# Later steps for batch 1's first-stage matmuls, an earlier step for M, in a kernel of an FFT filter and a two-branch maxout layer

## The chip, the cores and the metric

The kernel runs on one core of one Trainium2 chip. The core has a matrix engine (TensorE, PE in the profile, whose weight loads are PEld), a vector engine (DVE), a scalar engine (ACT), GpSimd (POOL) and a queue engine that only starts transfers (SP). Sixteen DMA engines move data between HBM and the on-chip memory SBUF. Matmuls write to PSUM, from which DVE or ACT copy ("evict") the result. Each engine executes its own instructions strictly in the order written, so one instruction that waits holds up all behind it on that engine. The metric is the device time of one execution in microseconds, as the median of several.

## The reference

```python
X = np.fft.rfft(x, axis=1)                    # x: 8 batches, 3072 rows, 256 channels
Y = X * (filt_r + 1j * filt_i)[None]
y = np.fft.irfft(Y, n=3072, axis=1)
x = y.reshape(24576, 256)
h1, h2 = x @ w1, x @ w2                        # 256 -> 1024
out = np.maximum(h1, h2) @ w_out               # 1024 -> 256
```

The kernel writes the maximum as max(h1, h2) = relu(h1 - h2) + h2. With Wd = w1 - w2 the first part needs one matmul into the hidden layer instead of two, and the second part is linear, so that h2 @ w_out = y @ M with M = w2 @ w_out, a 256x256 matrix that is made once.

## The kernel before

The transform of 3072 points is split into 96 x 32. Four stages make up the filter. The first multiplies with a 96-point table over the row index p (`f1` for batch 1, `s1` for batches 2 to 7, which fold pairs of rows first). The second (`s2`) does the 32-point part and the twiddle factors; its result is multiplied with the filter F (`product`, on DVE). The third (`s3`) goes back, and the fourth (`s4`) undoes the 96-point part and leaves y, transposed, for 384 rows at a time: one tile. Between the first and the second stage the data change their place across partitions by a round trip through DRAM: `f1` or `s1` store to `ad` (line 332 for batch 1, line 356 for others), and `f1_read` (line 338) or `s1_read` (line 362) reads it back as `bt`. Between the third and the fourth stage `zd` and `zr` do the same. Batch 0 alone goes through transposes on TensorE instead of these trips, in a prologue of about 38 us.

After the prologue comes one long loop over 64 tiles of 384 rows (8 per batch) and, in each tile, 8 steps. A step of the loop issues, in this order:

1. `moe_h(tt, j)`: two matmuls (line 448) that make the hidden block j of tile tt, and its eviction with the relu (line 450 on DVE or 452 on ACT);
2. what the table `mid` holds for this step: the visits, which do second and third stages of the next batch and first stages of the one after;
3. `moe_o(tt - 1, ...)`: three or four matmuls (line 480 with Wo, line 478 with M) into the output of the tile before;
4. what the table `todo` holds for this step, in the order in which it was planned;
5. after step 4 of a tile, `s4` (line 428) for the next tile.

Steps are numbered through a batch, 0 to 63; tile 0 has steps 0 to 7, in which there is no `moe_o` as no tile is before it. The planner is a list written out by hand: there are no costs or due times in it, and nothing is moved at run time.

What the change touches, all for the first two tiles and a little behind:

- `f1(1, c)` for c = 4 to 15: one matmul of 512 columns with C1 (line 324) on half of an input tile `xb`, an eviction to `at` (ACT, line 329, for even c; DVE, line 327, for odd c), and after each odd c a store of two c's to `ad` on SP. The calls for c = 0 to 3 stand before the loop. Input comes in three loads of POOL (line 88): c = 4 to 7 in `load_x(1, 2, 2)`, c = 8 to 11 in `load_x(1, 4, 2)`, c = 12 to 15 in `load_x(1, 6, 2)`. POOL issues the first, then the load of Wo (`load_wo`, line 288), then makes three quarters of Wd (line 292), and only then issues the other two, the last quarter of Wd and the casts of w2 (line 285).
- `prep_t(0)`, `prep_t(1)` at steps 7 and 8 transpose w2 (line 299, eviction on ACT, line 300), and `prep_m` multiplies it with Wo: 16 matmuls (line 306) and one eviction (line 308). M is first read by the last matmuls of an output block of tile 0, in `moe_o` at step 12.
- `f1_read(1)`: two transfers on SP that read `bt` of batch 1, each half of the frequencies; they wait for all stores to `ad`. The first second-stage matmuls of batch 1 (line 376) are in the visit at step 25, and they need the first of the two halves.
- `load_xf(2, c)`: the input of batch 2 in pieces, each two transfers on SP (line 93), and for c < 3 two small ones in between (line 97). `fold(2, c)` on POOL (lines 103 and 104) reads it, and `s1(2, c)` (line 349) at steps 25, 28, 31, ... reads the fold.

PSUM tiles for all but the output come from one ring of six (`ps`): an allocation waits for the eviction of the sixth before it.

Of the kernel before, what the change touches and what calls it, by code (L numbers as in the profile page):

```python
# [26 lines left out]
def kernel(  # L27
# [637 lines left out]
    def plan(b, step, fn, *a):  # L665
        todo.setdefault((b + step // 64, step % 64), []).append((fn, a))

    def plan_f1(b, nb, steps, read):
        for c, n in zip(range(4, 16), steps):
            plan(b, n, f1, nb, c, S if c % 2 == 0 else V)  # L670
        plan(b, read, f1_read, nb)
# [3 lines left out]
    def plan_f2(b, steps, quads, xs, folds):  # L675
        for n, st in enumerate(steps):
            mid.setdefault((b, st), []).append((visit, (b + 1, n, quads[n])))
        plan(b, steps[3] + 3, z_read, b + 1, 0)
        plan(b, steps[6] + 3, z_read, b + 1, 1)
        if b + 2 < B:  # L680
            for c in range(8):
                plan(b, xs[c], load_xf, b + 2, c)
                plan(b, folds[c], fold, b + 2, c)
            plan(b, steps[-1] + (6 if b else 11), s1_read, b + 2)
# [1 line left out]
    plan(0, 2, t2, 1, (V,))  # L686
    plan(0, 7, prep_t, 0)
    plan(0, 8, prep_t, 1)
    plan(0, 10, prep_m)
    for c in range(2, 8):  # L690
        plan(0, 8 * (c - 2) + 8, t2, c, (V,))
    plan_f1(0, 1, (1, 2, 5, 6, 9, 9, 10, 10, 11, 11, 12, 12), 13)
    plan_f2(0, (25, 28, 31, 35, 38, 42, 46), ((0,), (1,), (2,), (3,), (4,), (5,), (6, 7)),
            (9, 10, 14, 18, 21, 27, 30, 33), (16, 19, 25, 28, 31, 34, 38, 42))
    for b in range(1, B - 1):
        plan_f2(b, (7, 14, 18, 24, 31, 38, 42) if b > 1 else (14, 18, 24, 30, 34, 39, 42), ((0, 1), (2,), (3,), (4,), (5,), (6,), (7,)),
                range(-32, 32, 8) if b > 1 else range(-25, 31, 7), range(-22, 42, 8) if b > 1 else range(-15, 41, 7))
# [48 lines left out]
```

## Time and profile before

| | us |
|---|---|
| median of 3 runs | 503.3 (503.06 to 504.27) |
| the profiled execution, its own time | 506.75 |
| its span, first to last instruction | 504.9 |
| PE busy | 489.5 (97%) |
| DVE / ACT / POOL busy | 331.4 / 308.1 / 257.8 |
| loop starts (first `moe_h` on PE) | 38.66 |

Times below are microseconds from the start of the span of the profiled execution. In a timeline a line gives the start, the length, the engine, the line of the program, the operation and its tiles, and in brackets how long the engine sat idle before it and what released it. In a table by windows each row is one stretch: its length, the busy time of each engine with the number of instructions in brackets, then the clock that TensorE was granted as a share of full speed, the share of the DMA engines that was busy, and GB/s. Matmuls are pipelined, so the end of one and the start of the next overlap in the timeline; the distance from start to start is what a matmul costs in a stream.

### The profile page before, as it was taken

The numbers are of one execution on the slowest core, as the hardware profiler recorded it, in microseconds if no ns is written. First come the engines' busy times: TensorE is split into PE (matmuls) and PEld (weight loads), VectorE is DVE, ScalarE is ACT, GpSimd is POOL, SyncE is SP. The second block draws the span as 40 slices with busy tenths as digits, with TensorE's granted clock in tenths as the row PEclk, the third lists the DMA queues.
The fourth block names the chain that finished last, engine by engine and source line by source line (L and its number), as shares of the span: only waits on it lengthen the run. The fifth ranks groups of instructions, "written<-read, shape, count | busy, mean of one in ns | idle before, by whom it ended". The sixth has DMA issues, their size and how long they took to land.

```text
span 504.9 us, 13075 instructions
## 1 busy us (share of the span) xinstructions
PE 489.5 (97%) x5297; PEld 363.4 (72%) x5300; DVE 331.4 (66%) x514; ACT 308.1 (61%) x629; POOL 257.8 (51%) x342
## 2 busy tenths in 40 slices
PE   7788999999999999999999999999999999999996
PEld 3555767777777777777777777777777777777775
DVE  7785678557775687557764687557765687554552
ACT  5875477746774576547774676647774465544442
POOL 6695279566663755646645746528632221222220
PEclk9888999999999999999999999999999999999999
DMA  8989689997799659886779659796659235511112
GB/s 129 148 231 187 190 264 279 276 269 223 217 257 276 188 179 244 239 227 198 201 235 275 191 176 258 211 258 191 199 177 250 86 109 157 167 64 64 64 64 83
DMA packets 77966, 97.19 MB, mean 192 GB/s; under 512 B 8018, under 2 KB 54355, under 8 KB 77843
## 3 DMA queue, kind: packets, MB, share of 16 engines
q1 hardware_dynamic: 64642, 66.73, 49.5%
q0 software_dynamic: 13264, 29.64, 20.4%
q8 instruction: 41, 0.67, 0.6%
q14 instruction: 19, 0.15, 0.1%
HBM read 53.87 MB, written 47.19 MB: 200 GB/s over the span
## 4 chain that ended last, share of the span: by engine, by line
PE 90%; DMA 4%; POOL 3%; DVE 1%; issue 1%; ACT 0%; POOLq 0%
PE po L480 34%; PE ph L448 33%; PE po L478 8%; PE pz L399 5%; PE py L428 4%; DMA xb<-in_x_dram 3%; PE pa L349 2%; PE px L376 2%; POOL pq L382 1%; POOL xb L88 1%; PE pr L553 1%; PE pa L324 1%; DMA F<-in_filt_i_dram 1%; DVE F L130 0%; DVE pq L382 0%
## 5 line engine op out<-in xcount | busy, mean ns | idle before, releaser
L480 PE MATMUL po<-Wo,gt 128*128 128x256 bf16 x1536 | 261.0, 273 | 0.0
L452 ACT ACTIVATE gt<-ph 128x384 bf16<-128x384 f32 x321 | 157.0, 496 | 146.4 <-PE ph L448 145.7
L461 POOL DMA_DIRECT2D out_dram<-ot x186 | 102.6, 555 | 182.3 <-DVE ot L492 179.6
L480 PEld LDWEIGHTS <-gt 128*128 128x128 bf16 x1536 | 146.6, 98 | 66.0 <-issue 10.3
L450 DVE TENSOR_SCALAR gt<-ph 128x384 bf16<-128x384 f32 x191 | 104.9, 553 | 67.0 <-PE ph L448 63.8
L382 DVE TENSOR_TENSOR pq<-px,F 128x1024 bf16<-128x1024 f32 x91 | 106.9, 1218 | 23.2 <-PE px L376 22.7
L448 PEld LDWEIGHTS <-Wd 128*128 128x128 bf16 x1024 | 96.9, 98 | 12.4 <-issue 1.1
L103 POOL TENSOR_TENSOR xb<-XF 128x512 bf16<-128x512 f32 x48 | 61.2, 1275 | 45.6 <-DMA XF<-in_x_dram 35.5
L492 DVE COPY ot<-po 128x512 f32<-128x512 f32 x95 | 65.1, 685 | 25.2 <-PE po L480 24.1
L104 POOL TENSOR_TENSOR xb<-XF 128x512 bf16<-128x512 f32 x48 | 61.0, 1271 | 0.0
L353 ACT ACTIVATE at<-pa 128x512 bf16<-128x512 f32 x96 | 51.8, 610 | 2.4 <-PE pa L349 2.1
L403 ACT ACTIVATE zt<-pz 128x512 bf16<-128x512 f32 x84 | 45.6, 595 | 11.9 <-PE pz L399 9.7
L428 PE MATMUL py<-G,zr 96*128 96x96 bf16 x512 | 33.1, 207 | 0.2
L428 PEld LDWEIGHTS <-zr 96*128 96x128 bf16 x512 | 29.3, 98 | 2.7 <-DVE zr L556 0.4
L399 PE MATMUL pz<-pq,VP 64*64 64x256 bf16 x336 | 22.2, 281 | 0.1
L376 PE MATMUL px<-bt,U 64*64 64x256 bf16 x384 | 19.9, 275 | 1.2 <-ACT VQ L273 0.7
L399 PE MATMUL pz<-pq,VQ 64*64 64x256 bf16 x336 | 21.0, 269 | 0.0
L399 PEld LDWEIGHTS <-VP 64*64 64x64 bf16 x336 | 9.8, 105 | 13.6 <-issue 13.3
L349 PE MATMUL pa<-xb,CT 64*64 64x512 bf16 x192 | 19.5, 383 | 0.0
L376 PEld LDWEIGHTS <-U 64*64 64x64 bf16 x384 | 10.4, 107 | 4.1 <-issue 3.9
L563 PE MATMUL pd<-W 128*128 128x512 bf16 x28 | 10.5, 489 | 1.6 <-DVE zero L145 1.5
L349 PEld LDWEIGHTS <-CT 64*64 64x64 bf16 x192 | 8.7, 105 | 2.1 <-ACT gt L452 1.2
(429 smaller groups left out, 606.1 us busy)
## 6 DMA issues: line engine op xcount, KB each, us to landing
out_dram<-ot POOLq DMA_DIRECT2D x186, 128.0 KB, 3.4
XF<-in_x_dram SPq DMA_DIRECT2D x96, 192.0 KB, 5.1
ad<-at SPq DMA_DIRECT2D x56, 192.0 KB, 3.7
bt<-ad SPq DMA_DIRECT2D x14, 768.0 KB, 9.2
zd<-zt SPq DMA_DIRECT2D x42, 256.0 KB, 2.6
zr<-zd SPq DMA_DIRECT2D x56, 192.0 KB, 5.2
WS<-in_moe_w_dram SPq DMA_DIRECT2D x4, 512.0 KB, 7.1
xb<-in_x_dram POOLq DMA_DIRECT2D x8, 192.0 KB, 7.0
```

What stands on the lines that cost most here:

```text
L103: G.tensor_tensor(t_[:, 0], f[:, 0], f[:, 1], OP.add)
L104: G.tensor_tensor(t_[:, 1], f[:, 0], f[:, 1], OP.subtract)
L353: S.activation(at[:, m0:m0 + 2], pa[g], AF.Copy)
L382: E.tensor_tensor(pq, px.rearrange("p (o i) d -> p o i d", o=1).to_broadcast([128, 2, 2, D]), F[:, :, 2 * v:2 * v + 2, s], OP.mult)
L399: TE.matmul(pz[g][64 * s:64 * s + 64, i], tab[64 * g:64 * g + 64, 2 * v + i, s], pq[s][64 * g:64 * g + 64, q, i], start=(q == 0), stop=(q ...
L428: TE.matmul(py[:, m], zr[b][:, 4 * i + m, 128 * dc:128 * dc + 128], G1, start=True, stop=True)
L448: TE.matmul(ph, Wd[:, dc, 128 * j:128 * j + 128], y_[:, dc], start=(dc == 0), stop=(dc == 1))
L450: V.tensor_scalar(gt[tt][:, j], ph, 0.0, None, OP.max)
L452: S.activation(gt[tt][:, j], ph, AF.Relu)
L461: E.dma_start(out=dst, in_=ot[tt // 2][:, 3 * (tt % 2) + c])
L480: TE.matmul(p_, g_[:, n - 2, blk], Wo[:, n - 2], start=(e == 0), stop=(e == 9))
L492: V.tensor_copy(ot[tt // 2][:, e - 1:e + 1], po[q // 2 % 2])
```

## The change

The twelve first-stage calls of batch 1 that stand in the loop go from steps 1, 2, 5, 6, 9, 9, 10, 10, 11, 11, 12, 12 to steps 4, 5, 6, 7, 10, 10, 11, 11, 12, 12, 13, 13. The read of the exchange goes from step 13 to step 14. `prep_m` goes from step 10 to step 9. The first three pieces of batch 2's input are loaded at steps 10, 11 and 15 and no longer at 9, 10 and 14. What is computed, and on which engine, stays the same.

```diff
-    plan(0, 10, prep_m)
+    plan(0, 9, prep_m)
     for c in range(2, 8):
         plan(0, 8 * (c - 2) + 8, t2, c, (V,))
-    plan_f1(0, 1, (1, 2, 5, 6, 9, 9, 10, 10, 11, 11, 12, 12), 13)
+    plan_f1(0, 1, (4, 5, 6, 7, 10, 10, 11, 11, 12, 12, 13, 13), 14)
     plan_f2(0, (25, 28, 31, 35, 38, 42, 46), ((0,), (1,), (2,), (3,), (4,), (5,), (6, 7)),
-            (9, 10, 14, 18, 21, 27, 30, 33), (16, 19, 25, 28, 31, 34, 38, 42))
+            (10, 11, 15, 18, 21, 27, 30, 33), (16, 19, 25, 28, 31, 34, 38, 42))
```

## The prediction

> **What bounds the kernel now.** I read the page first: PE is busy 97% of the span, and the windows from 60 us on show it at 100%, so time is won only where PE stands still or runs slowly, and what is won there lasts unless something further on is late. Then the waits of PE from the loop's start to 80 us, to find the places; then windows of 3.41 us for the clock; then the timelines of PE and SP around the steps that move, and the transfers' times to landing.
>
> ```profile
> PE 489.5 (97%) x5297; PEld 363.4 (72%) x5300; DVE 331.4 (66%) x514; ACT 308.1 (61%) x629; POOL 257.8 (51%) x342
> ...
> PE pa L324 <- DMA xb<-in_x_dram: 2.2, 1, 2.2
> ...
> 8.49:11.90 3.41, 1.72 (x18) 0.69 (x15) 3.23 (x11) 1.83 (x6) 1.14 (x3) 0.99 1.07 181
> 11.90:15.31 3.41, 3.41 (x27) 2.29 (x27) 1.36 (x2) 2.81 (x6) 1.57 (x3) 0.51 1.10 178
> ...
> 18.72:22.13 3.41, 2.52 (x94) 1.91 (x92) 3.11 (x5) 3.41 (x7) 2.33 (x6) 1.00 1.03 138
> 22.13:25.55 3.42, 1.20 (x78) 0.79 (x56) 3.21 (x3) 2.79 (x6) 2.22 (x3) 0.99 0.96 171
> 25.55:28.96 3.41, 2.75 (x108) 1.71 (x98) 3.09 (x3) 2.24 (x5) 3.41 (x2) 0.51 0.87 196
> ...
> 39.20:42.61 3.41, 1.21 (x11) 0.63 (x9) 0.88 (x3) 0.89 (x2) 3.41 (x5) 0.99 1.17 140
> 42.61:46.02 3.41, 3.41 (x22) 2.18 (x21) 2.79 (x5) 1.17 (x3) 2.51 (x5) 0.51 1.14 265
> ```
>
> The wait is `f1(1, 4)` of step 1: its load lands at 41.7, and PE has stood since 39.55. The windows show a second cost. Three times a window in which PE was busy for 1.72 us or less is followed by one at a granted clock of 0.51; after a window with 2.52 busy the clock stayed at 1.00. The stall of step 1 is one of the three. From 42.01 to 47.06 PE took 5.05 us for work that at the full-clock distances takes 3.39 (six `ph` pairs at 0.326, one transpose group 0.445, three `f1` at 0.217, `py` 0.34): 1.66 us lost.
>
> The queue that matters later is SP, and the first use of what it reads:
>
> ```profile
> 51.31 0.30 SPq L332 DMA_DIRECT2D ad<-at  x1
> 51.66 0.42 SPq L93 DMA_DIRECT2D XF<-in_x_dram  x1
> 52.13 0.44 SPq L97 DMA_DIRECT2D XF<-in_x_dram  x1
> ...
> 54.25 0.32 SPq L332 DMA_DIRECT2D ad<-at  x1
> 54.62 0.43 SPq L93 DMA_DIRECT2D XF<-in_x_dram  x1
> ...
> 56.62 0.83 SPq L332 DMA_DIRECT2D ad<-at  x2
> 60.07 1.35 SPq L338 DMA_DIRECT2D bt<-ad  x2
> ...
> DMA to landing us min/median/max: 5.7/6.9/8.0
> ...
> 66.39 0.41 PE L376 MATMUL px<-bt,U 64*64 64x256 bf16 x8
> ```
>
> The first half of `bt` lands at 60.07 + 5.7 = 65.77, and PE uses it at 66.39: 0.62 us of slack, in a stretch where PE is full. Anything that brings PE here earlier without bringing `bt` earlier ends in a wait.
>
> **The change part by part.** Start PE at 39.39, where the next matmul could follow the first two `ph`.
>
> *Step 1 to 4, c = 4.* Now `ph` of steps 2, 3, 4 and the transposes of step 2 come before it: 3 x 0.326 + 0.445 = 1.42 us of work, until 40.81. Their inputs are there: POOL has the third quarter of Wd, which step 4 needs, at 40.24 (36.50 + 3.74), and the ring's six-back evictions end at 39.45 or before. The load is not earlier, since POOL's order isn't touched, so `f1(1, 4)` still starts at 41.75. The stall shrinks from 2.20 to 0.78 us: 1.42 won. In the window 39.20 to 42.61 PE is then busy 1.21 + 1.42 = 2.63, above the 2.52 that kept the clock: 1.66 won more.
>
> *Steps 5 to 8.* `py`, `ph`, `f1`, `ph`, `f1`, `ph`, transposes of w2, `f1`, and `ph` of tile 1 run at full clock from 41.97 to 44.72. Steps 6 and 7 need the last quarter of Wd (POOL, 42.49), step 7 the first cast of w2 (43.44): both there. ACT and DVE have two or three evictions of 0.5 to 0.7 queued, within the ring. Then `moe_o` of step 8 needs Wo. It was issued at 35.56 and took 9.9, so it lands at 45.46; the kernel before came here at 47.83 and never saw it. New stall: 0.78 us (bounds: nothing if Wo takes as long as its neighbours' 6.7 to 7.9, 1.3 if half a microsecond more; I take its own row). PE is busy 2.6 us in that window, so the clock should hold.
>
> *M a step sooner.* The second transposes of w2 now run at 45.94, ACT's copy (1.03) ends at about 47.6, and `prep_m` starts there, about 0.1 behind what PE could do: 0.1 lost. Its 16 matmuls (1.75) and M's eviction are the same work; M is ready at 50.2, two steps before its use. The first pair of step 10, `f1(1, 8)` and `(1, 9)`, starts at 50.16 against 49.92 before, since it now stands behind `prep_m`; its load landed at 40.16 + 7.1 = 47.3, the next at 40.68 + 7.9 = 48.6. No wait.
>
> *Sum to step 14:* 1.42 + 1.66 - 0.78 - 0.1 = 2.2 us won. Step 14's `ph`, at 56.69 before, comes at about 54.45.
>
> *SP.* Here the gain is given back. The store of c = 8, 9 was issued 1.39 after its matmuls began, so it now goes at 51.55 against 51.31. Behind it SP issues, in the same order as before, the four transfers of batch 2's piece 0 (1.85 us), a store, the four of piece 1 (1.9), two stores and the read: moving loads and stores by a step each keeps them in line. The 0.74 in which SP waited for the store of c = 10, 11 (54.25) goes, as that eviction is now done by 52.7. So the last store goes out at 56.63 instead of 57.06: only 0.43 earlier, although PE is 2.2 earlier. With the landing as before (some 2.95) the read is issued at 59.64 and its first half lands at 65.35. PE is there at 66.39 - 2.2 = 64.2. New stall: 1.2 us, and the gain there is 1.0 (bounds: 0.8 less stall if the read takes 0.5 to 0.8 less, because POOL's output writes of 59.43 and 60.0 are over sooner; 2.6 more if it takes the 8.3 of the fastest later read, in a fuller stretch; I take its own 5.7 with a little off).
>
> *What comes back after that.* Before, DVE was still at a copy and a relu when `px` was ready: product at 67.25, 0.86 after `px` began, against 0.43 at 74.34. PE then lost some 0.3 us at 69.64, waiting for it. With a PE stall ahead, DVE is free: 0.3 comes back, so 1.3.
>
> *Batch 2's piece 2*, a step later behind the same read, is issued right after it and lands the same 0.43 earlier. Its fold ended at 73.65 and `s1(2, 2)` used it at 74.56, a slack of 0.9; with the 0.43 that caps the gain there at 1.3, or 1.8 if the read is 0.5 faster. Pieces 0 and 1 are folded on POOL 5 us ahead of use, so the later issue costs nothing; without that cover a piece would cost the 2.5 us of a fold. Later exchanges have 2.4 us (batch 2: read at 102.93, landing up to 11.8, use at 117.30) and 4 us of slack (batch 3), so what is left reaches the end.
>
> So 1.3 by the rows as they stand, up to 1.8 with a somewhat quicker read; I take 1.5. On the profile's own 506.75 that is 505.25. The median of the runs shown is 3.45 lower; 1.85 of the 506.75 lies outside the span, and where the rest is the trace doesn't say. I take the difference over: 503.3 - 1.5 = 501.8.
>
> **Rule against row.** The row is the stall of 2.2 us with the clock at 0.51 in the window behind. The Trainium skill, "TensorE: Matmul & The Clock Gate", section on why this matters for your kernels, says to avoid idle gaps above about 3 us, which would leave a 2.2 us gap without a price. The windows here disagree: 1.7 to 2.2 us of idle in 3.41 sufficed three times. By that rule the sum to step 14 would be 0.54.
>
> **Rivals.**
> 1. *The read is quick, and nothing catches up.* All 2.2 stay: 501.1. For it: PE's whole gain is measured rows, and the read of `bt` has 0.26 MB less output traffic beside it. Against: slack 0.62.
> 2. *The clock is lost again, at step 25 (the other side).* A stall of 1.2 leaves PE busy 2.2 of 3.41 us, between the 1.72 that lost the clock and the 2.52 that kept it, so no row decides. It does from about 1.7 of idle at the latest. Price: 1.66. At that point: 2.2 - 1.7 + 0.3 - 1.66 = -0.9, so 504.2; at a stall of 1.2, 503.6.
> 3. *The half clock of 42.6 has another cause and stays, or is absent in unprofiled runs.* Then 1.42 - 0.78 - 0.1 = 0.54 is won; PE reaches step 25 within the slack, no new stall: 502.8. Against: the three pairs of windows. (This is also where the Trainium skill's rule above would put the time.)
> 4. *Wo lands later or earlier,* 44.7 to 46.8: it moves the first sum by +0.8 to -1.3, but step 25 takes up nearly all of it, so it changes little: counted within the forecast.
>
> **How the numbers follow.** A 0.3% change, 1.5 us, is about what a measurement of this kernel can tell from none. Forecast (won 1.0 to 1.9) 0.5; rival 1, 0.2; rival 2, 0.2; rival 3, 0.1. The range leaves out the worse half of rival 2 and holds the rest: 500.9 to 503.8. The forecast alone is 501.4 to 502.3. Faster by over 0.3%: 0.3 of the forecast, whose middle lies on the line, and all of rival 1: 0.5. Slower by over 0.3%: rival 2 with a stall beyond 2 us, or a read as long as the later ones: 0.13. Within: 0.37.
>
> **What would show it.** Right: PE's wait at line 324 falls to about 0.8 at 41.75 and the clock stays at 1.00 through 47; a wait of about 0.8 for Wo at line 480 at 45.5; step 14 about 2.2 earlier; SP's last store near 56.6 and a wait of 0.8 to 1.2 for `bt` at line 376 near 65. Wrong: the clock at 0.5 anywhere behind 38 us, no wait at line 376, or a `bt` read of over 7 us for its first half.

## The result

| | before | after |
|---|---|---|
| median of 22 runs each, us | 503.41 (501.77 to 506.40) | 505.29 (503.54 to 508.69) |
| ratio after / before | | 1.0039, 95% interval 1.0022 to 1.0056 |
| profiled execution, its own time, us | 506.75 | 504.60 |
| its span, us | 504.9 | 502.8 |

The kernel became slower by 0.39%, about 1.9 us. The forecast was 501.8, faster by 0.3%. The two profiled executions show the opposite sign: the span after is 2.1 us shorter. Both facts are true, and the way from one to the other is what this case teaches. Two executions timed later, one of the kernel before at 1005.08 us and one of xf_early at 1752.72, were far slower than all others and stand outside every ratio and count below.

The views of the profile after that answer to those shown of before: PE's busy line, the waits of PE, windows of 3.41 us (length; busy us of PE, PEld, DVE, ACT, POOL with counts; granted clock; DMA share; GB/s), SP's timeline with the landing of the two halves of the read, and the first use of `bt`.

```profile
PE 487.1 (97%) x5297; PEld 361.1 (72%) x5300; DVE 331.3 (66%) x514; ACT 308.3 (61%) x629; POOL 259.4 (52%) x342
...
PE px L376 <- DMA bt<-ad: 2.0, 1, 2.0
...
PE po L480 <- DMA Wo<-in_moe_w_out_dram: 0.5, 1, 0.5
...
PE pa L324 <- DMA xb<-in_x_dram: 0.4, 1, 0.4
...
39.20:42.61 3.41, 2.96 (x28) 1.76 (x28) 2.50 (x5) 2.63 (x7) 3.41 (x4) 1.00 1.24 248
42.61:46.02 3.41, 2.90 (x33) 2.35 (x32) 1.64 (x3) 2.34 (x4) 0.84 (x4) 1.00 1.06 236
59.07:62.48 3.41, 3.09 (x29) 2.20 (x26) 1.30 (x2) 1.71 (x4) 3.39 (x5) 1.00 0.59 170
62.48:65.89 3.41, 1.68 (x22) 1.17 (x23) 1.77 (x4) 1.01 (x3) 0.99 (x2) 1.00 1.13 353
65.89:69.30 3.41, 3.29 (x50) 2.28 (x48) 2.47 (x3) 3.00 (x8) 0.00 (x0) 1.00 1.08 323
...
49.52 0.30 SPq L332 DMA_DIRECT2D ad<-at  x1
49.87 0.42 SPq L93 DMA_DIRECT2D XF<-in_x_dram  x1
...
51.83 0.35 SPq L332 DMA_DIRECT2D ad<-at  x1
52.23 0.43 SPq L93 DMA_DIRECT2D XF<-in_x_dram  x1
...
54.21 0.83 SPq L332 DMA_DIRECT2D ad<-at  x2
58.90 1.18 SPq L338 DMA_DIRECT2D bt<-ad  x2
...
DMA to landing us min/median/max: 5.3/6.3/7.4
...
64.21 0.41 PE L376 MATMUL px<-bt,U 64*64 64x256 bf16 x8 [2.04 <-DMA bt<-ad]
```

The load wait of 2.2 us at line 324 is 0.4, the clock stays at 1.00 through 46, a wait of 0.5 us for Wo is new, and PE now waits 2.04 us for `bt` at step 25. These are the effects that were forecast; the last was forecast at 1.2. So the suspicion falls on the profiled execution of before: it may not stand for the rest.

The way to see it in a span is to cut it at two marks: the first `ph` of the loop on PE, and the first `px` of step 25. From the second mark to the end ten of these thirteen executions take 438.5 to 438.7 us, and up to the first mark all these kernels issue the same instructions; the loop's start alone lies anywhere from 37.0 to 40.6 us.

| execution | loop start | first `px` of step 25 | start to `px` | `px` to end |
|---|---|---|---|---|
| before (the page shown ahead) | 38.66 | 66.39 | 27.7 | 438.5 |
| b_again (kernel before) | 38.52 | 62.42 | 23.9 | 438.6 |
| b_look2 (kernel before) | 38.14 | 61.92 | 23.8 | 438.6 |
| b_look3 (kernel before) | 40.64 | 64.35 | 23.7 | 438.6 |
| after | 37.00 | 64.21 | 27.2 | 438.6 |
| after_again (kernel after) | 37.26 | 65.59 | 28.3 | 439.8 |
| late8 | 38.89 | 69.70 | 30.8 | 438.7 |
| first4 | 38.46 | 63.01 | 24.6 | 439.5 |
| first4_again (first4) | 40.31 | 64.23 | 23.9 | 438.6 |
| first4_m9 | 37.69 | 63.67 | 26.0 | 439.2 |
| xf_early | 37.56 | 62.32 | 24.8 | 438.7 |
| m9_xf | 37.19 | 63.00 | 25.8 | 438.5 |
| m9_xf_again (m9_xf) | 37.90 | 62.49 | 24.6 | 438.6 |

Three of four profiled executions of the kernel before take 23.7 to 23.9 us for this stretch, and the one on which the prediction was built takes 27.7. Against that one the kernel after won 0.5 us here (27.2), where the forecast had 1.0 at this point; the rest of its shorter span is the loop's start, 37.00 against 38.66, which the change doesn't touch.

### The profile page after: what moved, and what is told of

The parts are those of the page before. It is cut to its first block, busy times and chain, and to the rows that moved or that the text cites. A ratio compares the mean times of both kernels' runs of the same rounds, so it can differ in the third digit from the quotient of the medians.

```text
span 502.8 us, 13075 instructions
## 1 busy us (share of the span) xinstructions
PE 487.1 (97%) x5297; PEld 361.1 (72%) x5300; DVE 331.3 (66%) x514; ACT 308.3 (61%) x629; POOL 259.4 (52%) x342
## 4 chain that ended last, share of the span: by engine, by line
PE 88%; DMA 7%; POOL 3%; issue 1%; SPq 0%; ACT 0%; DVE 0%; POOLq 0%; ACTq 0%
PE po L480 33%; PE ph L448 32%; PE po L478 8%; PE pz L399 5%; PE py L428 4%; PE pa L349 2%; PE px L376 2%; DMA Wo<-in_moe_w_out_dram 2%; DMA xb<-in_x_dram 2%; DMA bt<-ad 1%; DMA ad<-at 1%; DMA F<-in_filt_r_dram 1%; DMA F<-F 1%; POOL pq L382 1%; POOL xb L88 1%
## 5 line engine op out<-in xcount | busy, mean ns | idle before, releaser
L563 PE MATMUL pd<-W 128*128 128x512 bf16 x28 | 9.3, 442 | 1.8 <-DVE zero L145 1.5
```

## The experiments

The theory that the texts below call 1, E or A is one, refined as results came: the load wait of step 1 and its half clock are in some executions only, and the kernel after pays a wait for `bt` in all of them, because SP's order makes the read late. Theory 2 is that every execution of before has the load wait; the other rivals (B, C, D) are stated where they are tested. The runs of the experiments were made on three chips, each with the kernel before timed beside them: b_again, first4, late8 and readfirst on the first, xf_early, first4_m9, m9_xf and after_again on the second, the others on the third.

**The kernel before, three times more.** No edit; b_again was also timed twelve times, the others are single executions.

> The kernel before, unchanged, once more. Theory 1 (the profiled execution of before was a slow one: its loop lost 1.66 us to the half clock behind the 2.2 us load wait, which most executions don't pay): the median stays near 503.4, the executions scatter over several us, and a profile near the median shows no granted clock of 0.5 between the loop's start and step 14, or a load wait well under 2.2 us. Theory 2 (every execution pays it, and the kernel after loses the same or more elsewhere): the profile again shows a wait of about 2.2 us at line 324 and a clock of 0.5 behind it.

> One more look at the kernel before. Theory E (the load of c = 4 to 7 lands anywhere between 4.8 and 6.7 us after its issue, so the wait at step 1 is anything from 0 to 2.2 us and the half clock follows only the long ones): a third value for the wait; if it is over 1.5 us the next window of 3.41 us is at about 0.5, if under 1 us the clock stays at 1.00. Theory 2 (the profile before was the rule): 2.2 us again.

> The same once more, for the same question: how often the load is late. Under theory E about four looks in ten show a wait of over 1.5 us (11 of 27 timed executions of before on the first chip lay above 504), under theory 2 all.

Measured: median of b_again 503.21 (ratio 0.9993, 0.9967 to 1.0018); the single executions 502.25 and 504.68. The windows of b_again around the loop's start, with the same columns as above:

```profile
35.80:39.21 3.41, 2.93 (x26) 1.48 (x24) 2.60 (x5) 2.44 (x6) 3.41 (x4) 1.00 0.96 142
39.21:42.63 3.42, 3.42 (x32) 2.18 (x31) 3.25 (x7) 2.48 (x6) 3.42 (x5) 1.00 1.27 224
42.63:46.04 3.41, 3.41 (x40) 2.71 (x39) 1.92 (x5) 3.23 (x5) 1.90 (x5) 1.00 1.08 203
```

and the timeline of PE in b_look2, where `f1(1, 4)` follows the two `ph` without a gap:

```profile
38.14 0.89 PE L448 MATMUL ph<-y__990,Wd 128*128 128x384 bf16 x4
38.86 0.38 PE L324 MATMUL pa<-xb,C 96*96 96x512 bf16 x1
39.08 0.49 PE L448 MATMUL ph<-y__990,Wd 128*128 128x384 bf16 x2
```

None of the three has the load wait or a half clock behind it. The load took 4.8, 4.6 and 4.6 us to land, against 6.7 in the first profile; in b_again it was issued at 34.42, so it landed at 39.2, just when PE asked at 39.25. In b_look3 PE was 2 us late itself, after a half clock in the prologue from 33.8 to 40.6 us; it shows that an execution of 504.68 need not have the load wait. Theory 1, in the form of theory E, holds: the stall that the change removes is present in some executions. Theory 2 falls.

How often the stall is there can't be read from the timed runs, since they have no trace. One of four profiled executions of before had it, and so did late8, whose order is the same up to there. The other traces say a little more, as all kernels issue this load at the same place ahead of the loop. The order of before asks for it 0.73 us behind the loop's start (39.25 in b_again). It landed 3.0 us behind that start in before and late8, 2.7 in the first profile of after, 2.4 to 3.7 in all four profiled executions on the second chip, 1.9 in first4 and 1.4 in m9_xf_again; in the other five it landed 0.7 us behind the start or sooner. By these rows the order of before would have waited in nine of fourteen executions, the second chip's among them. That is argued and not shown, since no execution of before was profiled on that chip; but its timed executions of before were slower than elsewhere, with a median of 504.68.

**The first part alone.** On the kernel before, only c = 4 to 7 move.

```diff
-    plan_f1(0, 1, (1, 2, 5, 6, 9, 9, 10, 10, 11, 11, 12, 12), 13)
+    plan_f1(0, 1, (4, 5, 6, 7, 9, 9, 10, 10, 11, 11, 12, 12), 13)
```

> Only the first part of the change: c = 4 to 7 at steps 4, 5, 6, 7, all else as before (c = 8 to 15 at 9 to 12, read at 13, M at step 10, loads of batch 2 at 9, 10, 14). Theory 1: the loss of the kernel after comes from the second part, which makes the read of the exchange late; then this kernel is not slower than before (502 to 503.5) and its wait for bt at step 25 is under 1.2 us, since the SP queue gets the store of c = 8, 9 some 2 us earlier than in the kernel after. Rival (moving c = 4 to 7 itself costs, by the waits for Wo at step 8 or by a half clock at step 25): as slow as the kernel after, 504.5 to 505.5.

> first4 (only c = 4 to 7 moved) timed again beside before on this chip. Theory E: its fastest executions equal before's fastest (no load wait there to remove), and its slow tail is thinner, so the median is 0.4 to 1.5 us lower: 502.3 to 503.3. Rival (first4 gains nothing): the medians agree within 0.3 us.

Measured: 502.77 (ratio to before 0.9986, 0.9964 to 1.0009) and, again, 503.28 (0.9977, 0.9950 to 1.0004). Neither profile shows a wait for `bt` at step 25; a wait for Wo of 0.24 us shows in the first. (That execution has a tail of 439.5: batch 2's read came 0.5 us late at 115 us, a place where I had counted on 2.4 us of slack.) The first part does no harm, and the rival of the first text falls. Of 24 executions five lay above 504 us, of the 64 of before on the same occasions 26; the fastest are equal, 501.80 and 501.55. That fits the removal of an occasional stall, but each ratio's interval holds 1, and b_look3 was above 504 without the stall.

**The second part alone.** On the kernel before:

```diff
-    plan(0, 10, prep_m)
+    plan(0, 9, prep_m)
...
-    plan_f1(0, 1, (1, 2, 5, 6, 9, 9, 10, 10, 11, 11, 12, 12), 13)
+    plan_f1(0, 1, (1, 2, 5, 6, 10, 10, 11, 11, 12, 12, 13, 13), 14)
...
-            (9, 10, 14, 18, 21, 27, 30, 33), (16, 19, 25, 28, 31, 34, 38, 42))
+            (10, 11, 15, 18, 21, 27, 30, 33), (16, 19, 25, 28, 31, 34, 38, 42))
```

> Only the second part: c = 8 to 15 a step later, read at 14, M at step 9, loads of batch 2 a step later; c = 4 to 7 at the old steps 1, 2, 5, 6. Theory 1: the read goes out later than before while PE is no earlier, so a wait for bt of 0.5 to 1.5 us appears at step 25, and the time is 504 to 505.5. Rival: no loss by itself (503.4), since the read has 0.62 us of slack and PE no gain to give back.

Measured: 506.52, ratio 1.0052 (1.0026 to 1.0078), above the 504 to 505.5 expected. The two longest waits of PE:

```profile
PE pa L324 <- DMA xb<-in_x_dram: 2.1, 1, 2.1
PE px L376 <- DMA bt<-ad: 1.8, 1, 1.8
```

The second part alone makes a loss, without any gain of PE to give back: 1.8 us at step 25. The rival falls. The medians are 3.2 us apart, and this one trace doesn't show what the rest is in the timed executions. It also met the late load, and the clock then was 0.5 for two windows, from 41.1 to 47.9 us.

**The kernel after again.** No edit.

> The kernel after, unchanged, once more. Theory A: the wait for bt at step 25 is in every execution (1.5 to 2.5 us), while the load wait of step 4 is 0 to 1 us; the median is 505 to 505.6 and even the fastest execution is some 2 us behind the fastest of before. Theory D (the wait is there in some executions only, as the load wait of the kernel before was): the profile shows under 0.5 us at line 376.

Measured: 505.25, the fastest 504.15 (before's 501.85). Before had a median of 504.68 on this chip, and the ratio is 1.0014 (0.9991 to 1.0038): here no loss can be told from noise, as would be so if the order of before often met the late load on this chip. The wait for `bt` is there again, 1.98 us, so theory D falls. Here it was followed by the half clock, which it was not in the first profile. The windows, cut where the clock changes in this execution:

```profile
59.01:62.42 3.41, 3.41 (x34) 2.71 (x33) 1.43 (x3) 1.96 (x4) 3.39 (x5) 1.00 0.42 140
62.42:65.83 3.41, 1.43 (x22) 1.02 (x24) 1.53 (x3) 0.49 (x1) 2.50 (x4) 1.00 1.04 322
65.83:69.25 3.42, 3.42 (x24) 1.76 (x17) 2.35 (x2) 1.58 (x3) 0.00 (x0) 0.50 1.10 359
```

The wait lay from 63.6 to 65.6, inside one window, which left PE 1.43 us busy. In the first profile of after the clock changed at 21.52 and 28.34, and steps of 3.41 us from there put boundaries at 62.48 and 65.89: the three windows shown for it above. There the wait lay from 62.2 to 64.2, 0.3 of it ahead of a boundary, and the window was left with 1.68 us busy; the clock stayed at 1.00. `px` to end is 439.8 against 438.6, 1.2 us more. What decided between the two is not shown: how busy PE was in the window doesn't do it alone, since in b_look2 a window of the prologue with 2.19 us busy (18.33 to 21.75) was followed by a half clock. This execution also waited 2.2 us in all for Wd at steps 4 and 6, since POOL had waited 1.8 us for a load of w1 and w2 that SP issues; so late loads aren't gone; here it is another one.

**SP relieved by loading batch 2's pieces behind the read.** On the kernel after:

```diff
-            (10, 11, 15, 18, 21, 27, 30, 33), (16, 19, 25, 28, 31, 34, 38, 42))
+            (15, 15, 15, 18, 21, 27, 30, 33), (16, 19, 25, 28, 31, 34, 38, 42))
```

> The kernel after, with batch 2's pieces 0 and 1 loaded at step 15, behind the read of the exchange, and not at steps 10 and 11. Theory 1 (the eight transfers of these pieces on SP, 3.75 us of issue, make the last stores and so the read late): the last store goes out 2 us or more earlier, the wait for bt at step 25 falls from 2.0 to under 0.5 us, and the time is 502 to 503.5. Rival (the wait is not SP's issue but the landing of the stores and of the read, 3.3 and 5.3 us): the wait stays above 1.2 us and the time at 504.5 or more. Price in either: the folds of batch 2 may come late at step 25, up to 1 us.

Measured: 512.55, ratio 1.0174 (1.0143 to 1.0205). The read goes out at 55.54 and `px` starts at 62.27 without a wait, so the first half of theory 1 holds. My price was far off: PE then waits for the fold.

```profile
PE pa L349 <- POOL xb L103: 7.1, 1, 7.1
```

The pieces stand behind 1.5 MB of the read. I had allowed 1 us for what cost 7.7, with the clock at 0.5 from 65.3 to 75.6. The time says nothing for or against theory 1; the missing wait for `bt` does.

**SP relieved by loading them early.** On the kernel after:

```diff
-            (10, 11, 15, 18, 21, 27, 30, 33), (16, 19, 25, 28, 31, 34, 38, 42))
+            (7, 8, 15, 18, 21, 27, 30, 33), (16, 19, 25, 28, 31, 34, 38, 42))
```

> The kernel after, with batch 2's pieces 0 and 1 loaded at steps 7 and 8 (SP is idle there) and not at 10 and 11; piece 2, the first stages and the read stay as in the kernel after. Theory A (the loss of the kernel after is the wait for bt at step 25, and that comes from the two pieces standing on SP between the stores of the exchange): the last store goes out some 9 us after step 9's first matmul or earlier instead of 9.84, the read some 2 us sooner, the wait for bt falls from 2.04 to under 0.5 us, and the median falls from 505.3 to 503.5 or less. Rival B (the wait comes from the first stages being two steps' work later, behind M, whatever SP does): the wait stays above 1.2 us and the median above 504.5.

Measured: 503.18 without the one execution named above, 503.42 with it (ratio to before 0.9980, 0.9953 to 1.0006), with after_again at 505.25 beside it. SP's timeline shows the four stores together and the read behind them:

```profile
49.90 3.97 SPq L332 DMA_DIRECT2D ad<-at  x4
55.59 1.24 SPq L338 DMA_DIRECT2D bt<-ad  x2
...
62.32 0.41 PE L376 MATMUL px<-bt,U 64*64 64x256 bf16 x8
```

No wait at line 376 is left, and 2.1 us of the kernel after's time comes back with all its matmuls where they were (the ratio of the two medians is 0.9959, 0.9941 to 0.9987 by resampling their runs). Rival B falls: it is the eight transfers between the stores that make the lateness expensive. The last store goes out at 53.6, 8.5 behind step 9's first matmul (45.09), 1.4 sooner than in the kernel after; the read goes out 10.5 behind it, 3.5 sooner, more than expected, as the stores also land sooner.

**M's share.** first4 with M at step 9, and then with the pieces at steps 7 and 8 as well:

```diff
-    plan(0, 10, prep_m)
+    plan(0, 9, prep_m)
...
-            (9, 10, 14, 18, 21, 27, 30, 33), (16, 19, 25, 28, 31, 34, 38, 42))
+            (7, 8, 14, 18, 21, 27, 30, 33), (16, 19, 25, 28, 31, 34, 38, 42))
```

> The first four calls moved as in first4, and M made at step 9, so that c = 8 and 9 stand behind its 1.75 us of matmuls; everything else as before. Theory A: the stores run 1.0 to 1.75 us later than in first4, of which the slack before step 25 takes 0.6; a wait for bt of 0.3 to 1.0 us, median 503.0 to 504.0. Rival B: the same, so this run only sizes M's share; rival C (M's place matters by itself, through the wait for w2's copy): a wait on PE at line 306 of 0.3 us or more.

> first4_m9 with pieces 0 and 1 of batch 2 at steps 7 and 8. Theory A: no wait for bt at all, the read goes out 2 us earlier than in first4_m9, and the median is at or a little below first4's, 502.0 to 502.9. Against it: the pieces share the DMA engines with the input of c = 8 to 15 and with Wo, and a wait of 0.2 to 1 us for one of these would take the place of the one removed.

> m9_xf timed again on the same chip as first4. If the read of the exchange is no longer late in either, the two agree within 0.5 us; if the pieces loaded early hold up Wo (1.2 us of wait in its first profile against 0.24 in first4's), it is 0.5 to 1 us slower than first4.

Measured: first4_m9 504.75 against 503.25 for m9_xf beside it (ratios to before 1.0013, 0.9992 to 1.0035, and 0.9981, 0.9959 to 1.0002). Both lie above what was expected, on a chip where before stands at 504.68 (the texts expected 503.0 to 504.0 and 502.0 to 502.9). Waits of PE in first4_m9:

```profile
PE po L480 <- DMA Wo<-in_moe_w_out_dram: 0.8, 1, 0.8
PE px L376 <- DMA bt<-ad: 0.8, 1, 0.8
PE pa L349 <- POOL xb L104: 0.7, 1, 0.7
```

M alone, ahead of the stage's last eight matmuls, brings a wait of 0.8 us at step 25, of the 2.0 in the kernel after, and then 0.7 at the fold of piece 2. There is no wait at line 306, so rival C falls. With SP relieved both are gone. m9_xf waited 1.2 us for Wo in its first profile and not in its second; timed again it had 503.16 beside first4's 503.28, so the early pieces cost nothing that can be told, and the second expectation's worse branch falls.

So three versions without the wait for `bt` and with c = 4 later stand 0.5 to 1.5 us under before in five comparisons, and no single one is clear of it. That they beat before is likely and not settled; that they beat the kernel after is clear for xf_early and m9_xf, whose runs stood beside it (m9_xf: 0.9960, 0.9941 to 0.9975, by the same resampling).

## Why the prediction was wrong

The step that failed is the first of the sum, "Step 1 to 4, c = 4": 1.42 us from the stall and 1.66 from the clock, taken as the property of the kernel and not of one execution. In the other three profiled executions of before both are 0. Without them the sum to step 14 is -0.78 - 0.1 and not +2.2. The mechanism itself was right: where the load is late, as in the first profile and in late8, the wait is 2.1 to 2.2 and the half clock follows. A second term was mis-sized: the wait for `bt`, put at 1.2, was 2.0 in both profiles of after. For this reason the kernel after, even against the slow execution of before, had won only 0.5 at step 25 and not 1.0.

The evidence was on the table. The profiled execution stood at 506.75, 3.45 above the median. I put 1.85 of this down to what lies outside the span, but every execution has that much (1.8 in the profile after), so it explains no difference; of the rest I wrote that the trace doesn't say where it is, and took it over to the forecast. The 3.45 was in all likelihood the very thing that I then counted as a gain: 27.7 against 23.8 us to step 25 is 3.9. Rival 3 came near ("or is absent in unprofiled runs"), but kept the load wait and dropped only the clock, and so still won 0.54.

Point by point:

- *The wait for Wo, 0.78 forecast:* between 0 and 1.2 us in the profiles with c = 4 later, 0.51 in the first of after. Right in kind; it too varies with the landing.
- *PE at step 14 some 2.2 earlier:* its `ph` stands 15.4 us behind the loop's start in the profile after (52.39) and 18.0 in the profile before: right, 2.6, between these two. In b_again it stands 14.2 behind (52.71): against an execution without the load wait the change makes step 14 later by 1.2.
- *SP, "Here the gain is given back":* right, and it is the cause of the loss. The last store left 9.84 us behind step 9's first matmul (54.7 and 44.86) against 7.9 before (57.06 and 49.16): 1.94 later relative to PE, where the prediction had 1.77.
- *"With the landing as before (some 2.95)":* mis-sized. From the last store to the read it is 4.2 us after (54.7 to 58.90) against 3.0 before. In all four profiles in which SP issued the eight transfers and the stores back to back (both of after, late8, first4_m9) it is 4.0 to 4.3; in before, b_again and first4, with a pause of 0.6 to 0.7 us ahead of the store of c = 10, 11, it is 3.0 to 3.2; in xf_early, without the transfers, 2.0. By these rows the pause that I counted as saved had let the queue drain. That it is the backlog, and not the output writes that now fall beside it (POOL at 55.1), is argued and not shown apart. With the read 0.4 quicker (5.3 against 5.7) this gives 1.2 + 1.2 - 0.4 = 2.0, the measured wait.
- *Rival 2, the half clock at step 25:* happened in one of two profiles of after. The prediction placed its onset between 1.72 and 2.52 us busy in a window; cut where the clock changes, the traces show no such line. The half clock followed windows with 1.43 (after_again), 1.94 (late8, 37.70 to 41.12) and 2.19 (b_look2), and did not follow 1.68 (after) or 2.14 (late8, 68.42 to 71.84).
- *What comes back:* 0.3 forecast by an idle DVE. In the profile after, `pz` runs from 67.05 to `px` at 67.51, 0.46, without the 0.3 of before, as said. It doesn't show in the span, as `px` to end takes 438.6 after and 438.5 before.
- *The Trainium skill's rule* ("TensorE: Matmul & The Clock Gate", section on why this matters for your kernels: avoid idle gaps above about 3 us): three waits here disagree, as 2.0 to 2.2 us cost a half clock in before, late8 and after_again; two cost none, 2.04 in after and 1.82 in late8 at step 25. The same page's section on the clock gate says that the window runs freely and doesn't start with the kernel; with that the traces agree: the clock fell at 25.49 and 42.56 in before and at 24.05 and 41.12 in late8, both times 17.07 apart, five times 3.41, but 1.44 earlier in the one than in the other. So the window from 39.20 to 42.61, in which the prediction counted PE's busy time, belongs to that one execution.

From the loop's start to step 25 an execution of before without the late load takes 23.7 to 23.9 us, and the first profile of after 27.2: 3.4 lost, 1.2 of it by step 14 (0.5 for Wo, 0.4 for the load at line 324, the rest not followed up), 2.0 at `bt`, and in one of the two profiles of after another 1.2 of half clock behind it. Against an execution with the late load, 27.7, the change wins 0.5. The medians say 1.9 lost, between the two.

## What to carry to other kernels

Before a stall is counted as a gain, hold the profiled execution against the median: if it is slower by about the price of that stall, the stall may be what makes it slow, and other executions may have nothing to give. A few more profiles of the same kernel tell. A transfer that nothing waits for still occupies its queue: stores that a later read depends on should not stand between bulk loads, and loading the bulk into an idle stretch (here three steps earlier) gave back 2.1 us. Moving work later on the producing side has to be measured at the first use of what it produces, with the landing times of the queue as it will be then.

## What the runs showed of the hardware

The same load of 384 KB, issued at the same place, landed after 4.6 to 4.8 us in three executions of before and after 6.7 in a fourth; 7.3 in one of after. The clock changed only at whole steps of 3.41 us from its other changes in the same execution. A TensorE wait of about 2 us cost itself alone (after, 2.04) or another 1.2 to 1.7 us of half clock (after_again, before), and in late8 the clock stayed at 0.5 for two windows; what decides is open. And a pause of 0.6 to 0.7 us among the issues of a queue went with a read that could start 1 us sooner behind the last store (3.0 to 3.2 against 4.0 to 4.3), with the same bytes to move.
